# Loading q and k nine rows of a head at a time, and putting the rows back in order after the transposes

## The chip, the cores and the metric

The kernel runs on one core of one Trainium2 chip. The metric is the device time of one execution in microseconds (us). Executions agree within about 1%, so differences of a few us are judged on several runs taken in alternation with the kernel before. "Span" is the time from the first to the last instruction in the profiled execution; it is about 2 us shorter than the device time.

In what follows PE is the matrix engine, DVE the vector engine, ACT the scalar engine, POOL the GpSimd engine and SP the sync engine. DMA engines move data between the chip's main memory (HBM) and SBUF, the memory that the compute engines work from; PSUM is where PE leaves its results. A piece is a contiguous run of bytes that a load leaves in SBUF, and a packet is one entry of the trace's record of what the DMA engines moved; here each piece of q and k is one packet.

## The reference, cut to what matters

```python
# q, k, v: [8 batches, 8 heads, 576 rows, 64] float32;  w_phi: [64, 128]
proj = x @ w_phi                                   # for q and for k
proj = proj - max(abs(proj), axis=-1)
phi  = concatenate([exp(proj), exp(-proj)])        # 256 features
kv, z = sum_s phi_k * v,  sum_s phi_k
attn  = (phi_q @ kv) / (phi_q @ z + 1e-6)          # x: [8, 576, 512]
X = rfft(x, axis=1)[:, :64]                        # 64 modes
Y = X * (w_r + 1j*w_i)                             # w_r, w_i: [64, 512, 512] float32, 134 MB together
u = x + irfft(Y);  out = u + relu(u @ w_ch)
```

## The kernel before

One core does everything. 16 units (4 groups of two heads x 4 pairs of batches) go through the attention; a software pipeline overlaps three units. The spectral weights arrive in 64 groups, each of two 512 KB loads (bf16 after the cast in the load), in eight buffers plus five borrowed places, and are used ("mixed") between the pieces of the attention from the fifth unit on. POOL issues every load that casts float32 to bf16: k, q and the weights, in program order.

```python
def load(t, src, g, bp, eng):            # k, q by POOL; v by SP
    for i in range(2):                   # batch of the pair
        hs = src[2 * bp + i, 2 * g:2 * g + 2]
        eng.dma_start(                   # rows 4p..4p+3 on partition p
            t[:, 8 * i:8 * i + 8, :].rearrange("p (h c) d -> p h (c d)", h=2),
            hs[:, 0:512, :].rearrange("h (p c) d -> p h (c d)", c=4))
        eng.dma_start(                   # the other 64 rows
            t[64 * i:64 * i + 64, 16:18, :],
            hs[:, 512:576, :].rearrange("h p d -> p h d"))
# [cut] turn(): nine 128x128 transposes on PE, two ACT copies out of PSUM
# [cut] the attention of a unit; then, behind the attention and interleaved with it:
def wload(g, mg):
    wt = home(g, mg)
    for i, w in ((0, moe_w_r), (1, moe_w_i)):
        pool.dma_start(wt[:, i], w[mg*MG:(mg+1)*MG, g*128:(g+1)*128, :].rearrange("m p e -> p m e"))
    return wt
# [cut] the output stage: for each pair of batches nine chunks of 128 rows, and
            if n in (3, 7):
                nc.sync.dma_start(       # 1 MB, 128 partitions
                    out[2 * bp + n // 4, 0:512, :].rearrange("(p c) e -> p c e", c=4),
                    of[n // 4])
```

A q or k load thus leaves 512 B per piece in SBUF (four rows of 64 bf16) and the remainder loads 128 B.

## Time and profile before

| what | before |
|---|---|
| device time, median of the first 3 runs | 490.25 us |
| span | 488.5 us |
| load stage (start to the first matmul of the output stage) | 447.5 us |
| output stage (from there to the end) | 41.0 us |
| waits of PE for k | 25.0 us |

The last row is from the view of waits (engine, its output tile and line, what it waited for, us in total, times, longest; `one` is a tile in PSUM, L38 the line of a helper that issues every operation):

```profile
PE one L38 <- DMA kb<-in_k_dram: 25.0, 9, 8.7
```

The page of the kernel before gives the engines' busy tenths in 40 slices of 12.2 us, the data moved in each slice, the packets by queue (q0 is POOL's, q1 is SP's), and the chain of work that ended last:

```profile
PE   2772787778887887787696629676667767656994
...
DVE  5776569779767877868859544752222112100874
...
DMA  9999999999999999999999999999999999992576
GB/s 170 193 216 216 203 214 206 200 203 155 218 218 213 143 205 213 183 204 207 210 190 176 218 165 205 206 207 206 207 206 214 213 213 217 213 214 45 226 296 252
DMA packets 112341, 98.63 MB, mean 202 GB/s; under 512 B 17968, under 2 KB 110768, under 8 KB 111280
...
q0 software_dynamic: 94736, 77.09, 100.5%
q1 hardware_dynamic: 17568, 21.04, 14.5%
...
DMA 40%; DVE 23%; PE 22%; ACT 5%; issue 4%; POOL 3%; another core or an unknown queue 0%; DVEq 0%; SPq 0%; ACTq 0%; POOLq 0%
```

The DMA row is full through slice 36 (about 440 us); the rows of PE and DVE, the busiest compute engines, are not. The chain agrees: 40% of the span is DMA. So the load stage is a transfer stage. The GB/s row counts bytes written (bf16), and about 210 is what the loads reach at most of the time. The row has dips below it (155, 143, 183, 176, 165), which the prediction reads as holes in which the DMA engines ran short of work. The DMA digits can't show them, since packets overlap, but the packet records do: the packets that started in the microsecond from 164 us took 0.28 us of 16 engines' time, where the stretch with weights alone (330 to 350 us) has 1.24.

The transfers by tile in the same kernel (issuing queue, number of loads, KB each, median us from issue to landing):

```profile
out_dram<-of SPq DMA_DIRECT2D x8, 1024.0 KB, 3.9
kb<-in_k_dram POOLq DMA_DIRECT2D x32, 128.0 KB, 12.0
qb<-in_q_dram POOLq DMA_DIRECT2D x32, 128.0 KB, 7.9
...
kb<-in_k_dram POOLq DMA_DIRECT2D x32, 16.0 KB, 11.6
```

Each unit takes four loads for k and four for q. From the view of the tile that collects the output sums, the first and last start of its matmuls (us) show where the output stage begins:

```profile
L596 PE MATMUL pt<-xs,ident_b x36: 376/379/631, 447.5 to 480.8; 128*128 128x512 bf16 x36
```

The packet count of q0 agrees exactly with arithmetic: 64 weight groups, the channel weights, k and q make 90,624 data packets, and 257 loads by POOL add one 4-byte completion packet on each of 16 engines (257 x 16 = 4,112): 94,736 together.

### The profile page before, as it was taken

Reading aid. Unit: us, or ns where it says so; the run is one execution under the profiler, and the core shown is the slowest. Engines: PE = TensorE matmul, PEld = TensorE weight load, DVE = VectorE, ACT = ScalarE, POOL = GpSimd, SP = SyncE. Lnnn points to the kernel's source line nnn. Section 1 sums busy time; section 2 is a strip of 40 time slices with the busy share of each in tenths; the row PEclk is TensorE's granted clock in tenths of the full one; section 3 lists DMA queues with packets and bytes.
Section 4 is the critical chain, followed back from the end, with each engine's and each line's share of the span. In section 5 each row is a group of like instructions: output and inputs, shape, how many; then the busy total and the mean of one; then the engine's idle time right before and its main releaser. Section 6 shows DMA issues by size and latency. Waiting matters only on the chain.

```text
span 488.5 us, 8037 instructions
## 1 busy us (share of the span) xinstructions
PE 347.6 (71%) x3104; PEld 212.3 (43%) x3133; DVE 284.4 (58%) x492; ACT 256.8 (53%) x435; POOL 181.7 (37%) x267
## 2 busy tenths in 40 slices
PE   2772787778887887787696629676667767656994
PEld 1451655555565555554464416442333333322441
DVE  5776569779767877868859544752222112100874
ACT  3770866866966875765575717421213323210763
POOL 8754344647442642644255244232332323100000
PEclk9996958888977986978788957778999999975998
DMA  9999999999999999999999999999999999992576
GB/s 170 193 216 216 203 214 206 200 203 155 218 218 213 143 205 213 183 204 207 210 190 176 218 165 205 206 207 206 207 206 214 213 213 217 213 214 45 226 296 252
DMA packets 112341, 98.63 MB, mean 202 GB/s; under 512 B 17968, under 2 KB 110768, under 8 KB 111280
## 3 DMA queue, kind: packets, MB, share of 16 engines
q0 software_dynamic: 94736, 77.09, 100.5%
q1 hardware_dynamic: 17568, 21.04, 14.5%
q8 instruction: 24, 0.39, 0.3%
q14 instruction: 13, 0.11, 0.1%
HBM read 163.64 MB, written 9.44 MB: 354 GB/s over the span
## 4 chain that ended last, share of the span: by engine, by line
DMA 40%; DVE 23%; PE 22%; ACT 5%; issue 4%; POOL 3%; another core or an unknown queue 0%; DVEq 0%; SPq 0%; ACTq 0%; POOLq 0%
DMA wt<-in_moe_w_i_dram 28%; PE one L38 12%; DMA wt<-in_moe_w_r_dram 9%; DVE va L38 6%; DVE mq L38 4%; PE pt L596 4%; DVE nd L38 4%; DVE mk L38 4%; DMA kb<-in_k_dram 3%; DVE xs L38 3%; PE two L38 3%; POOL wt L38 3%; PE pt L598 3%; ACT AB L38 2%; DVE rd L38 1%
## 5 line engine op out<-in xcount | busy, mean ns | idle before, releaser
L38 ACT ACTIVATE AB<-two 128x1024 bf16<-128x1024 f32 x64 | 62.1, 1022 | 50.7 <-DVE mk L38 50.3
L38 ACT ACTIVATE AQ<-two 128x1024 bf16<-128x1024 f32 x64 | 62.5, 1038 | 18.0 <-PE two L38 12.3
L38 POOL DMA_DIRECT2D wt<-in_moe_w_r_dram x59 | 44.7, 758 | 66.8 <-DMA wt<-in_moe_w_r_dram 29.1
L38 POOL DMA_DIRECT2D qb<-in_q_dram x64 | 42.2, 666 | 73.4 <-DMA wt<-in_moe_w_i_dram 31.1
L38 POOL DMA_DIRECT2D wt<-in_moe_w_i_dram x59 | 44.5, 754 | 53.9 <-DMA wt<-in_moe_w_i_dram 48.8
L38 PE MATMUL one<-va,AB 128*128 128x65 bf16 x512 | 45.8, 223 | 17.5 <-DVE va L38 17.3
L465 ACT CAST xw<-one 128x512 bf16<-128x512 f32 x36 | 21.1, 586 | 67.4 <-PE one L463 51.2
L38 POOL DMA_DIRECT2D kb<-in_k_dram x64 | 42.3, 672 | 38.3 <-DMA wt<-in_moe_w_i_dram 17.9
L460 DVE COPY xT<-one 128x512 bf16<-128x512 bf16 x36 | 15.3, 425 | 61.8 <-PE one L458 61.1
L463 PE MATMUL one<-wchb,xT 128*128 128x512 bf16 x135 | 38.2, 397 | 14.5 <-DVE xT L460 14.0
L38 DVE TENSOR_REDUCE mk<-two 128x8 f32<-128x1024 f32 x32 | 39.0, 1219 | 5.8 <-PE two L38 5.8
L38 DVE TENSOR_TENSOR va<-vn,ee 128x1152 bf16<-128x1152 f32 x32 | 42.0, 1355 | 0.0
L38 PEld LDWEIGHTS <-AB 128*128 128x128 bf16 x512 | 29.1, 112 | 27.3 <-DVE va L38 11.9
L38 DVE TENSOR_REDUCE mq<-two 128x8 f32<-128x1024 f32 x32 | 37.7, 1217 | 1.4 <-PE two L38 1.4
L38 PE MATMUL one<-kvz,AQ 128*128 128x65 bf16 x512 | 29.6, 205 | 6.9 <-ACT kvz L38 2.7
L38 PE MATMUL one<-ident_b,kb 128*128 128x128 bf16 x144 | 14.4, 244 | 25.3 <-DMA kb<-in_k_dram 24.4
L38 PEld LDWEIGHTS <-AQ 128*128 128x128 bf16 x512 | 25.7, 105 | 15.1 <-issue 12.1
L38 PE MATMUL one<-CF,xs 128*128 128x256 bf16 x160 | 30.9, 364 | 1.7 <-DVE xs L38 1.7
L38 PE MATMUL one<-wt,XT_70 128*32 128x512 bf16 x256 | 22.5, 427 | 13.0 <-DMA wt<-in_moe_w_i_dram 8.9
L38 DVE TENSOR_TENSOR nd<-one,nd 128x390 f32<-128x390 f32 x48 | 27.1, 565 | 5.4 <-PE one L38 0.5
L609 DVE TENSOR_TENSOR of<-pt,rl 128x512 f32<-128x512 f32 x32 | 21.8, 690 | 13.8 <-ACT rl L607 13.4
L38 PE MATMUL two<-w2blk,qT 128*128 128x256 bf16 x128 | 19.8, 289 | 13.0 <-ACT AB L38 10.6
(124 smaller groups left out, 638.0 us busy)
## 6 DMA issues: line engine op xcount, KB each, us to landing
wt<-in_moe_w_r_dram POOLq DMA_DIRECT2D x59, 512.0 KB, 15.6
wt<-in_moe_w_i_dram POOLq DMA_DIRECT2D x59, 512.0 KB, 17.8
vn<-in_v_dram SPq DMA_DIRECT2D x32, 256.0 KB, 7.3
out_dram<-of SPq DMA_DIRECT2D x8, 1024.0 KB, 3.9
kb<-in_k_dram POOLq DMA_DIRECT2D x32, 128.0 KB, 12.0
qb<-in_q_dram POOLq DMA_DIRECT2D x32, 128.0 KB, 7.9
vn<-in_v_dram SPq DMA_DIRECT2D x32, 32.0 KB, 7.5
yacc<-in_moe_w_r_dram POOLq DMA_DIRECT2D x2, 512.0 KB, 6.9
```

The source lines that it names most:

```text
L38: ins = f(*args, **kwargs)
L460: nc.vector.tensor_copy(xT, pt)
L463: nc.tensor.matmul(pf, lhsT=xT[:, g, :], rhs=wchb[:, g, :], start=(g == 0), stop=(g == 3))
L465: nc.scalar.copy(xw[:, bp, n, :], pf)
L596: nc.tensor.matmul(po, lhsT=ident_b, rhs=base, start=True, stop=False)
L598: nc.tensor.matmul(p, lhsT=CI[:, n % 4, :], rhs=src[:, 2 * bp + n // 4, :], start=False, stop=True)
L609: nc.vector.tensor_tensor(out=o, in0=ps[0], in1=rl, op=ALU.add)
```

## The change

The intent is fewer and longer packets. With nine rows of a head on a partition, 576 = 64 x 9 rows fit on 64 partitions, the two batches fill 128, and there is no remainder load: 1,152 B per piece and two loads instead of four for each of k and q. The price is that the transposes deliver rows in another order, so the ACT copies out of PSUM put them back into chunks of 128 rows, and v, the Fourier tables and the output take the new row order (row 9p + 4u + c on partition 64u + p), which splits v's loads and the output's stores into halves of 64 partitions.

The main parts of the edit:

```diff
         def load_v(self):
             self.vn = pin.tile([128, 18, D_], F32, name="vn")
-            load(self.vn, v, self.g, self.bp, sp)
+            for i in range(2):
+                vs = v[2 * self.bp + i, 2 * self.g:2 * self.g + 2].rearrange(
+                    "h (p r) d -> p h r d", r=9)
+                for u in range(2):
+                    sp.dma_start(
+                        self.vn[64 * u:64 * u + 64, 8 * i:8 * i + 8, :].rearrange(
+                            "p (h c) d -> p h (c d)", h=2),
+                        vs[:, :, 4 * u:4 * u + 4, :].rearrange("p h c d -> p h (c d)"))
+                sp.dma_start(self.vn[64 * i:64 * i + 64, 16:18, :], vs[:, :, 8, :])
+
+        def load_wide(self, src, name):
+
+            t = pin.tile([128, 2, 10, D_], BF16, name=name)
+            for h in range(2):
+                pool.dma_start(
+                    t[:, h, 0:9].rearrange("p r d -> p (r d)"),
+                    src[2 * self.bp:2 * self.bp + 2, 2 * self.g + h].rearrange(
+                        "b (p r) d -> b p (r d)", r=9))
+            return t
 
         def turn(self, src, name):
 
-            dst = pm.tile([128, 9, 128], BF16, name=name, tag="xT", bufs=3)
-            flat = src.rearrange("p n d -> p (n d)")
-            for lo, hi in ((0, 4), (4, 9)):
-                ptr = one([128, hi - lo, 128], BF16)
-                for j in range(lo, hi):
-                    pe.transpose(ptr[:, j - lo, :], flat[:, j * 128:(j + 1) * 128], ident_b)
-                act.copy(dst[:, lo:hi, :], ptr)
-            return dst
+            dst = pm.tile([128, 2, 2, 2, 2, 64], BF16, name=name, tag="xT", bufs=3)
+            rest = pm.tile([128, 2, 128], BF16, name=name + "r", tag="xTr", bufs=3)
+            flat = src.rearrange("p h r d -> p h (r d)")
+            for h in range(2):
+                ptr = one([128, 6, 128], BF16)
+                for j in range(4):
+                    pe.transpose(ptr[:, j, :], flat[:, h, j * 128:(j + 1) * 128], ident_b)
+                if h == 1:
+                    for hh in range(2):
+                        pe.transpose(ptr[0:64, 4 + hh, :], flat[:, hh, 512:576], ident_b)
+                act.copy(
+                    dst[:, h].rearrange("p m b u s -> p u (m b) s"),
+                    ptr[:, 0:4].rearrange("p (u m) (b s) -> p u (m b) s", u=2, b=2))
+                if h == 1:
+                    act.copy(rest[0:64], ptr[0:64, 4:6])
+            return dst, rest
```

In the attention code (cut): the projection of the remainder rows takes two matmuls of 64 input rows instead of one of 128 for `rows`, and one instead of two for `cols`; the sums over k accumulate in another order. The output:

```diff
             if n in (3, 7):
-                nc.sync.dma_start(
-                    out[2 * bp + n // 4, 0:512, :].rearrange("(p c) e -> p c e", c=4),
-                    of[n // 4])
+                rows = out[2 * bp + n // 4].rearrange("(p r) e -> p r e", r=9)
+                for u in range(2):
+                    nc.sync.dma_start(
+                        rows[:, 4 * u:4 * u + 4, :], of[n // 4][64 * u:64 * u + 64])
         for i in range(2):
-            nc.sync.dma_start(out[2 * bp + i, 512:576, :], ofr[64 * i:64 * i + 64, :])
+            rows = out[2 * bp + i].rearrange("(p r) e -> p r e", r=9)
+            nc.sync.dma_start(rows[:, 8, :], ofr[64 * i:64 * i + 64, :])
```

More of the change, by code (lines that the diff above doesn't have):

```diff
@@ L88 @@
     pm = pm_cm.__enter__()
-    def load(t, src, g, bp, eng):
-        for i in range(2):
-            hs = src[2 * bp + i, 2 * g:2 * g + 2]
-            eng.dma_start(
-                t[:, 8 * i:8 * i + 8, :].rearrange("p (h c) d -> p h (c d)", h=2),
-                hs[:, 0:512, :].rearrange("h (p c) d -> p h (c d)", c=4),
-            )
-            eng.dma_start(
-                t[64 * i:64 * i + 64, 16:18, :],
-                hs[:, 512:576, :].rearrange("h p d -> p h d"),
-            )
     class Unit:
@@ L108, in load_k @@
         def load_k(self):
-            self.kb = pin.tile([128, 18, D_], BF16, name="kb")
-            load(self.kb, k, self.g, self.bp, pool)
+            self.kb = self.load_wide(k, "kb")
         def load_q(self):
-            self.qb = pin.tile([128, 18, D_], BF16, name="qb")
-            load(self.qb, q, self.g, self.bp, pool)
+            self.qb = self.load_wide(q, "qb")
         def load_v(self):
             self.vn = pin.tile([128, 18, D_], F32, name="vn")
-            load(self.vn, v, self.g, self.bp, sp)
@@ L142, in rows @@
                 ps = two([128, 8, 128])
-                for j in range(4):
-                    if by_head:
-                        o = ps[:, 2 * j:2 * j + 2, :]
-                    else:
-                        h, cc = j // 2, j % 2
-                        o = ps.rearrange("p (c h) f -> p c h f", h=2)[:, 2 * cc:2 * cc + 2, h, :]
-                    pe.matmul(o, lhsT=tT[:, 4 * i + j, :],
-                              rhs=w2blk.rearrange("p (c f) -> p c f", c=2),
-                              start=True, stop=True)
+                o = ps.rearrange("p (h m e) f -> p h m e f" if by_head
+                                 else "p (m e h) f -> p h m e f", h=2, m=2)
+                for h in range(2):
+                    for m_ in range(2):
+                        pe.matmul(
+                            o[:, h, m_],
+                            lhsT=tT[0][:, h, m_, i].rearrange("p u s -> p (u s)"),
+                            rhs=w2blk.rearrange("p (e f) -> p e f", e=2),
+                            start=True, stop=True)
             else:
                 ps = one([128, 2, 128])
-                pe.matmul(ps.rearrange("p h f -> p (h f)"), lhsT=tT[:, 8, :], rhs=w2blk,
-                          start=True, stop=True)
+                for h in range(2):
+                    pe.matmul(ps[:, h, :], lhsT=tT[1][0:64, h, :], rhs=w2blk[0:64, 0:128],
+                              start=True, stop=True)
             n = slice(8 * i, 8 * i + 8) if i < 2 else slice(16, 18)
@@ L193, in kv @@
             pk = one([128, 4, 65])
-            for h in range(2):
-                for ab in range(2):
-                    o = pk[:, 2 * h + ab, :]
-                    for c in range(4):
-                        pe.matmul(
-                            o, lhsT=self.AB[i][:, ab, 4 * h + c, :],
-                            rhs=self.va[:, ab, 8 * i + 4 * h + c, :],
-                            start=(c == 0), stop=False,
-                        )
-                    r = slice(64 * i, 64 * i + 64)
+            hab = [(h, ab) for h in range(2) for ab in range(2)]
+            for h, ab in hab:
+                for c in range(4):
                     pe.matmul(
-                        o, lhsT=self.AB[2][r, ab, h, :], rhs=self.va[r, ab, 16 + h, :],
-                        start=False, stop=True,
-                    )
+                        pk[:, 2 * h + ab, :], lhsT=self.AB[i][:, ab, 4 * h + c, :],
+                        rhs=self.va[:, ab, 8 * i + 4 * h + c, :],
+                        start=(h == ab == c == 0), stop=False,
+                    )
+            r = slice(64 * i, 64 * i + 64)
+            for h, ab in hab:
+                pe.matmul(
+                    pk[:, 2 * h + ab, :], lhsT=self.AB[2][r, ab, h, :],
+                    rhs=self.va[r, ab, 16 + h, :], start=False, stop=(h == ab == 1),
+                )
             act.copy(self.kvz[:, i], pk)
@@ L219, in cols_q @@
             if i < 2:
-                ps = two([128, 2, 4, 128])
-                for c2 in range(2):
+                ps = two([128, 2, 2, 2, 128])
+                for e in range(2):
                     pe.matmul(
-                        ps[:, c2].rearrange("p n s -> p (n s)"),
-                        lhsT=w2blk[:, c2 * 128:(c2 + 1) * 128],
-                        rhs=self.qT[:, 4 * i:4 * i + 4, :].rearrange("p n s -> p (n s)"),
+                        ps[:, e], lhsT=w2blk[:, e * 128:(e + 1) * 128],
+                        rhs=self.qT[0][:, :, :, i].rearrange("p h m u s -> p h m (u s)"),
                         start=True, stop=True,
@@ L229, in cols_q @@
                 ps = one([128, 2, 128])
-                for h in range(2):
-                    pe.matmul(ps[:, h, :], lhsT=w2blk[:, h * 128:(h + 1) * 128],
-                              rhs=self.qT[:, 8, :], start=True, stop=True)
+                pe.matmul(ps, lhsT=w2blk[0:64, 0:128], rhs=self.qT[1][0:64],
+                          start=True, stop=True)
             self.pa = ps
@@ L238, in exp_q @@
             if i < 2:
-                t = pm.tile([128, 2, 2, 4, 128], BF16, name="AQ")
+                t = pm.tile([128, 2, 2, 2, 2, 128], BF16, name="AQ")
             else:
@@ L256, in num @@
                             pn[ab][:, n - n0, :],
-                            lhsT=self.AQ[i][:, ab, c % 2, 2 * h + c // 2, :],
+                            lhsT=self.AQ[i][:, ab, c % 2, h, c // 2, :],
                             rhs=self.kvz[:, i, 2 * h + ab, :], start=True, stop=True,
@@ L305 @@
     si = const.tile([128, 5], I32, name="si")
-    pool.iota(si[:, 0:4], [[1, 4]], base=0, channel_multiplier=4)
-    pool.iota(si[0:64, 4:5], [[1, 1]], base=512, channel_multiplier=1)
-    pool.iota(si[64:128, 4:5], [[1, 1]], base=512, channel_multiplier=1)
+    for u in range(2):
+        pool.iota(si[64 * u:64 * u + 64, 0:4], [[1, 4]], base=4 * u, channel_multiplier=9)
+        pool.iota(si[64 * u:64 * u + 64, 4:5], [[1, 1]], base=8, channel_multiplier=9)
     mi = const.tile([128, 64], I32, name="mi")
@@ L610 @@
             if n in (3, 7):
-                nc.sync.dma_start(
-                    out[2 * bp + n // 4, 0:512, :].rearrange("(p c) e -> p c e", c=4),
-                    of[n // 4])
+                rows = out[2 * bp + n // 4].rearrange("(p r) e -> p r e", r=9)
+                for u in range(2):
+                    nc.sync.dma_start(
+                        rows[:, 4 * u:4 * u + 4, :], of[n // 4][64 * u:64 * u + 64])
         for i in range(2):
-            nc.sync.dma_start(out[2 * bp + i, 512:576, :], ofr[64 * i:64 * i + 64, :])
+            rows = out[2 * bp + i].rearrange("(p r) e -> p r e", r=9)
+            nc.sync.dma_start(rows[:, 8, :], ofr[64 * i:64 * i + 64, :])
     pb_cm.__exit__(None, None, None)
```

## The prediction

> **What bounds the kernel now.** The transfers. On the page all slices up to about 440 us show the DMA engines at nine tenths or more while no compute engine stays there. The chain of waits gives DMA 40% of the span, nearly all of it from 217 us to 442 us and nearly all weights (wt). Before that the chain runs through DVE, PE and ACT at about 17.5 us a unit; after 447 us some 41 us of output remain, which the change hardly touches. The waits view shows POOL waiting 160 us in all for earlier weight loads to land before it may issue the next load, so DMA work saved is mostly time saved.
>
> **Packet costs.** The trace's packet records: a 1 KB weight packet takes 98 ns, a 512 B k/q packet 60, a 128 B one 32. Packets overlap: in the weights-only stage 4,014 packets start per 20 us on 16 engines, so one costs an engine about 80 ns. Scaling, my estimates are 48 ns for 512 B and 26 ns for 128 B.
>
> **Removed.** q and k are now 16,384 + 8,192 packets (50 + 13 us of all 16 engines). After: 8,192 packets of 1,152 B, estimated at 87 ns, 44.5 us. With 64 fewer completions that is about 19 us less DMA work. POOL issues 64 loads instead of 128 (670 ns each).
>
> **How much is on the path.** Until the first mix (108 us) compute sets the pace: the 13 weight groups loaded ahead just finish there, so the saving for units 0 to 6 is lost. Nine units remain, 1.2 us each: 11 us. Second, the DMA has short holes in the attention stage (around 112-116, 165-170, 247, 264 and 292 us, some 9 us together), where POOL's limited number of loads in flight consists of small q and k pieces. Half as many pieces should fill most holes. Third, the waits of PE for kb (16 us from 240 to 290 us) shrink with it.
>
> **Added.** Per turn one more ACT copy (existing ones 604-766 ns, so about 0.25 us net), one more transpose, per unit one more rows matmul for each of q and k; about 0.3 us per unit, partly hidden. v and the output are halved into 64 partitions: same packets, more issues (SP has time); a slight slowdown of v is possible.
>
> **A doubt.** The new loads have the batch (2) as outermost source dimension. The Trainium skill, "DMA: Bandwidth & Descriptors", section "Why a DMA increments its semaphore by 16 and not by 1", says the engine count divides the outermost dimension of both sides; then each q/k load runs on 2 of 16 engines (64 x 87 ns = 5.6 us) and 8 loads cover all. Nothing in the trace before shows this. Total work is unchanged, but engines go out of step by up to 5.6 us and first units start 1 to 2 us later. I count 3 us for it.
>
> **Sum.** 11 + 6 saved, less 3 for uneven engines, less 3 for added compute and v: about 11 us, so 479 us (range 467 to 490). Faster by over 2% 0.56, within 2% 0.39, slower 0.05.
>
> **Right if:** q0 packets fall from 94,736 to about 77,300; the last weight lands near 430 us instead of 442; the span of the output stage stays at 41 us; POOL's DMA busy time halves for qb and kb; PE's waits for kb shrink.
>
> **Wrong if:** rows of 1,152 B cost far more than 87 ns or are split; two-engine loads delay weights and kb, with PE waiting for kb longer than before; 64-partition v loads slow down; or units grow by more than 0.5 us, so that compute, not DMA, sets the pace and the saving turns into idle DMA.

## The result, and the profile after

The changed kernel takes 510.88 us (median of 4 runs, 507.64 to 512.73) against 490.7 us for the kernel before in the same comparison: ratio 1.0416, 95% interval 1.0346 to 1.0485, so 4% slower. A ratio is the mean time of one kernel's fast runs over that of the other's of the same rounds, so it is not quite the ratio of the medians. Executions over 1.5% slower than the fastest of the same kernel are left out of the means. The prediction (479, 467 to 490) missed.

The same lines of the page after:

```profile
PE   0674776786967497698558739766676767639990
...
DVE  4379488778777857967748656661221222103770
...
DMA  7999999999999999999999999999999999961997
GB/s 112 188 188 199 208 200 206 197 202 133 198 205 212 171 188 211 190 201 196 207 201 178 219 181 201 206 206 207 206 207 213 216 213 216 211 126 34 258 252 214
DMA packets 152918, 98.87 MB, mean 194 GB/s; under 512 B 66736, under 2 KB 151344, under 8 KB 151856
...
q0 software_dynamic: 134672, 77.31, 99.5%
q1 hardware_dynamic: 18208, 21.05, 16.2%
...
DMA 70%; PE 14%; DVE 5%; issue 3%; ACT 3%; POOL 2%; DVEq 0%; POOLq 0%; ACTq 0%
```

Two things stand out. The DMA row is still full and the chain is now 70% DMA. And q0 does not have the predicted 77,300 packets but 134,672, more than before, although the bytes are the same: "under 512 B" went from 17,968 to 66,736.

```profile
vn<-in_v_dram SPq DMA_DIRECT2D x64, 128.0 KB, 7.6
out_dram<-of SPq DMA_DIRECT2D x16, 512.0 KB, 5.8
kb<-in_k_dram POOLq DMA_DIRECT2D x32, 144.0 KB, 15.7
qb<-in_q_dram POOLq DMA_DIRECT2D x32, 144.0 KB, 14.2
```

```profile
L606 PE MATMUL pt<-xs,ident_b x36: 376/379/631, 460.0 to 493.9; 128*128 128x512 bf16 x36
```

The output stage starts at 460.0 us, 12.5 us later than before, and lasts 508.6 - 460.0 = 48.6 us, 7.6 us longer. So there are two losses, in two stages. (The half-size stores take 5.8 us to land, where the whole ones took 3.9.)

What the extra packets are, the trace's packet records say: 60,432 packets of POOL's queue are 4 B long. 129 of POOL's loads (the weights) account for 16 each, 2,064 together. The rest, 58,368, is 64 x 912, so every q or k load has 912 of them. And 912 = 14 x 64 + 16. A load of 128 pieces carried by two engines gives each 64 pieces; the count fits if each of the other 14 engines gets 64 four-byte packets in their place, and all 16 one completion packet. (By the same arithmetic a load carried by four engines would have 12 x 32 + 16 = 400.) The records do not name the engine, so the two engines are inferred from the count. The Trainium skill, "DMA: Bandwidth & Descriptors", section "Why a DMA increments its semaphore by 16 and not by 1", states the rule that gives two: the engine count must divide the slowest dimension of both sides, and the source here has the batch, 2, outermost. The page does not mention the four-byte packets.

### The profile page after: what moved, and what is told of

Read it like the earlier page. It is cut to its first block, busy times and chain, and to the rows that moved or that the text cites. A ratio compares the mean times of both kernels' runs of the same rounds, so it can differ in the third digit from the quotient of the medians.

```text
span 508.6 us, 8127 instructions
## 1 busy us (share of the span) xinstructions
PE 345.0 (68%) x3168; PEld 203.7 (40%) x3181; DVE 286.0 (56%) x492; ACT 260.6 (51%) x467; POOL 149.6 (29%) x204
## 3 DMA queue, kind: packets, MB, share of 16 engines
q0 software_dynamic: 134672, 77.31, 99.5%
## 4 chain that ended last, share of the span: by engine, by line
DMA 70%; PE 14%; DVE 5%; issue 3%; ACT 3%; POOL 2%; DVEq 0%; POOLq 0%; ACTq 0%
DMA wt<-in_moe_w_r_dram 22%; DMA wt<-in_moe_w_i_dram 22%; DMA kb<-in_k_dram 12%; DMA qb<-in_q_dram 7%; PE one L38 5%; DMA xs<-in_moe_w_r_dram 4%; PE pt L606 4%; DMA yacc<-in_moe_w_r_dram 3%; PE pt L608 3%; ACT AB L38 1%; DVE va L38 1%; DVE nd L38 1%; PE two L38 1%; POOL kb L38 1%; DVE mk L38 1%
## 5 line engine op out<-in xcount | busy, mean ns | idle before, releaser
L38 PE MATMUL one<-ident_b,kb 128*128 128x128 bf16 (+1 forms) x160 | 19.8, 275 | 48.3 <-DMA kb<-in_k_dram 48.0
L38 ACT COPY kT<-one 128x512 bf16<-128x512 bf16 x32 | 18.4, 597 | 43.7 <-PE one L38 42.9
L38 PE MATMUL one<-va,AB 128*128 128x65 bf16 x512 | 30.9, 226 | 13.5 <-DVE va L38 13.5
L38 POOL DMA_DIRECT2D qb<-in_q_dram x32 | 25.4, 797 | 46.9 <-DMA wt<-in_moe_w_i_dram 14.6
L38 POOL DMA_DIRECT2D kb<-in_k_dram x32 | 26.2, 821 | 37.1 <-PE one L38 14.0
L38 PEld LDWEIGHTS <-AB 128*128 128x128 bf16 x512 | 27.0, 120 | 18.6 <-issue 12.2
L38 PEld LDWEIGHTS <-kb 128*128 128x128 bf16 (+1 forms) x160 | 12.4, 121 | 54.9 <-DMA kb<-in_k_dram 50.9
L38 PEld LDWEIGHTS <-AQ 128*128 128x128 bf16 x512 | 23.8, 104 | 22.0 <-issue 19.5
```

The lines of the kernel that those rows point to most:

```text
L38: ins = f(*args, **kwargs)
```

## The experiments

Each kernel was timed in three rounds in alternation with the kernel before. "Load stage" and "output stage" are as defined above, from the profiled execution. The third column sums the duration of all packets that started before the last weight packet ended, divided by 16 engines; packets on one engine overlap, so it exceeds the elapsed time, and only its changes matter. It is my sum over the trace's packet records. The stage figures are each from one execution: between kernels whose loads are the same (before, e3, e4 and e5; or e1, e6 and e7) the load stage scatters by up to 2 us.

| kernel | load stage, us | packet time, us | of it 4 B packets of POOL | output stage, us | median, us | ratio to before |
|---|---|---|---|---|---|---|
| before | 447.5 | 538.3 | 4.7 | 41.0 | 490 | 1 |
| after | 460.0 | 555.1 | 40.2 | 48.6 | 510.88 | 1.0416 |
| e1_by_batch | 432.4 | 511.7 | 3.7 | 47.1 | 480.99 | 0.9814 |
| e2_before_batch_outer | 466.2 | 570.5 | 36.7 | 41.8 | 507.61 | 1.0355 |
| e3_before_out_halves | 446.9 | 538.7 | 4.7 | 48.6 | 496.56 | 1.0131 |
| e4_before_out_rows | 445.6 | | | 40.8 | 489.54 | 1.0000 |
| e5_before_out_evenodd | 446.2 | | | 42.5 | 491.82 | 1.0029 |
| e6_by_batch_two_queues | 431.3 | | | 44.8 | 478.11 | 0.9764 |
| e7_interleaved | 432.1 | 511.7 | 3.7 | 42.8 | 476.92 | 0.9730 |
| e8_after_out_whole | 461.8 | 553.7 | 38.9 | 43.2 | 506.82 | 1.0340 |
| e9_q_by_head | 448.5 | 539.0 | 20.7 | 49.0 | 498.47 | 1.0178 |
| e10_k_by_head | 449.2 | 538.0 | 20.9 | 49.0 | 500.23 | 1.0191 |

### e1_by_batch: the change with 64 as the outermost source dimension

```diff
-            for h in range(2):
-                pool.dma_start(
-                    t[:, h, 0:9].rearrange("p r d -> p (r d)"),
-                    src[2 * self.bp:2 * self.bp + 2, 2 * self.g + h].rearrange(
-                        "b (p r) d -> b p (r d)", r=9))
+            for b in range(2):
+                pool.dma_start(
+                    t[64 * b:64 * b + 64, :, 0:9].rearrange("p h r d -> p h (r d)"),
+                    src[2 * self.bp + b, 2 * self.g:2 * self.g + 2].rearrange(
+                        "h (p r) d -> p h (r d)", r=9))
```

> The changed kernel, but each q/k load takes one batch and both heads (64 partitions, outermost source dimension 64) instead of one head and both batches (outermost source dimension 2). Same number of loads, same 8,192 packets of 1,152 B. Theory A (batch-outermost loads run on two engines and make the other 14 carry 64 four-byte packets each): the four-byte packets of q0 fall from 60,432 to about 3,100, the load stage ends about 20 us earlier, time about 488 us, with the output stage still at 48 us. Rival B (rows of 1,152 B, 64-partition tiles or the added copies and matmuls are what costs): 505 us or more.

Measured: 480.99 us, ratio 0.9814 (0.9773 to 0.9854), faster by just under 2% and correct; that is 7 us below the expected 488, and the gain in the load stage was 27.6 us, not about 20. The same bytes land in the same places in the same number of pieces and loads; only which pieces share a load differs. From the page of this kernel and its views of transfers and of the output tile:

```profile
DMA  8999999999999999999999999999999999952997
GB/s 152 216 217 214 211 212 212 219 210 155 217 214 211 218 219 206 219 219 208 218 219 209 217 206 207 205 207 207 207 214 212 213 213 213 213 98 55 270 265 211
...
q0 software_dynamic: 77328, 77.08, 96.6%
```

```profile
out_dram<-of SPq DMA_DIRECT2D x16, 512.0 KB, 5.8
kb<-in_k_dram POOLq DMA_DIRECT2D x32, 144.0 KB, 14.6
```

```profile
L606 PE MATMUL pt<-xs,ident_b x36: 376/379/631, 432.4 to 465.7; 128*128 128x512 bf16 x36
```

q0 has 77,328 packets, the predicted "about 77,300" and exactly what the arithmetic gives (90,624 - 24,576 + 8,192 data packets and 193 x 16 completions). The load stage ends 27.6 us before that of the changed kernel and 15.1 us before that of the kernel before. The dips in the GB/s row between slices 11 and 24 are gone (in e6 and e7 too, while e3, e4 and e5 keep them), which was the second gain of the prediction. One dip is left (155, in the tenth slice): the stretch where the weight groups loaded ahead are done and the first mix, at 109.5 us, has not yet freed a buffer. There the saving of the first units turns into idle DMA, as predicted. The output stage is still 47.1 us, so it is a separate matter. Rival B falls: the longer pieces, 64-partition tiles, added copies and added matmuls all are in this kernel, and its load stage is the better one.

### e2_before_batch_outer: the outermost dimension alone, in the kernel before

Shortened:

```diff
+        # q and k only; v keeps its two loads
+            for h in range(2):
+                eng.dma_start(
+                    t[:, 16 + h, :],
+                    src[2 * bp:2 * bp + 2, 2 * g + h, 512:576, :])
```

The two remainder loads of 16 KB took one batch and both heads; here they take one head and both batches.

> The kernel before, but the two small remainder loads of q and k take one head and both batches (batch outermost) instead of one batch and both heads. Same number of loads and data packets. Theory A: 58,000 more four-byte packets, some 25 us more DMA work, time about 510 us, although no other part of the change is there. Rival B: 490 us, as before.

Measured: 507.61 us, ratio 1.0355 (1.0297 to 1.0414), 2.4 us under the expected 510. POOL's queue has 152,080 packets, 57,344 more than before (64 loads x 896):

```profile
q0 software_dynamic: 152080, 77.32, 103.2%
```

```profile
L603 PE MATMUL pt<-xs,ident_b x36: 376/379/631, 466.2 to 500.4; 128*128 128x512 bf16 x36
```

Nothing else of the change is present. These loads carry 16 KB where those of the change carry 144, and they still cost 18.7 us of load stage and 32.0 us of packet time in four-byte packets (36.7 - 4.7; the change: 36.5 over e1_by_batch). So the four-byte packets go with the number of pieces (128 a load) and the outermost dimension, not with the bytes.

### e9_q_by_head and e10_k_by_head: late k, or busy DMA engines?

A rival was still open. The changed kernel's PE waits much longer for k. The view of waits of the changed kernel, then of e1_by_batch:

```profile
PE one L38 <- DMA kb<-in_k_dram: 48.0, 12, 12.8
```

```profile
PE one L38 <- DMA kb<-in_k_dram: 12.1, 2, 7.8
```

One could say that a two-engine load of k is simply late, and that this is the loss. Then q, which PE hardly waits for, should be harmless. The edit, shortened:

```diff
+            if name == "qb":        # e9; "kb" in e10
                 # as in the change: one head, both batches
+            else:
+                # as in e1_by_batch
```

> The changed kernel with k loaded by batch (outermost source dimension 64) and only q still with the batch outermost. Theory A (the four-byte packets cost time on all DMA engines): half of them, about 31,800, so about half of the loss comes back: first output matmul at about 446 us, time 494 to 497 us, although PE's wait for kb shrinks to about that of e1_by_batch (12 us). Rival F (the loss is that kb lands late and PE waits for it, 48 us in the changed kernel against 12 us in e1_by_batch; q is hardly ever waited for): about 481 us.

> The mirror of e9: q loaded by batch, only k still with the batch outermost. Theory A: about the same as e9, 494 to 497 us. Rival F (late kb is the loss): about 510 us, as the changed kernel.

Measured: 498.47 us (ratio 1.0178, 1.0117 to 1.0239) and 500.23 us (1.0191, 1.0113 to 1.0269): the same within the noise, both somewhat past the middle between e1_by_batch and the changed kernel. Rival F needed 481 and 510. Part of the expectation missed. The two are 1.5 and 3.2 us above the range given, and in e9 PE's wait for kb was 27.7 us, not 12, although k is loaded there as in e1_by_batch. So k was late in e9 too, and e9 alone would not clear it. What does is that the length of this wait does not set the load stage. In e4 (below), whose loads are those of the kernel before, it was 9.4 us instead of 25.0, and the load stage is 445.6 us against 447.5:

```profile
PE one L38 <- DMA kb<-in_k_dram: 9.4, 3, 7.1
```

Nor is it the time that POOL needs to issue these loads. POOL was busy for 149.6 us in the changed kernel and for 135.7 in e1_by_batch, but for 181.7 in the kernel before, whose load stage is shorter than the changed kernel's; and in the changed kernel it waited more for transfers to land (203.9 us in all, against 162.5 in e1_by_batch).

What is left is occupation of the DMA engines, and the packet records show it. I counted from start and duration how many packets were in flight. Between 15 and 300 us of the changed kernel it was 19.9 on average, as many as in its stretch with weights alone (330 to 350 us, 19.9), so the engines were no less busy; but only 17.8 of them were data (over 4 B), against 19.1 of 19.4 in e1_by_batch. And the loss builds up only while q and k are loaded: against e1_by_batch, the 500th 1 KB packet of POOL's queue ended 5 us later, the 20,000th 17 us, the 40,000th (at 316.0 us) 27.5 us, and the 66,000th still 27.7 us.

### e3, e4, e5: what lengthens the output stage

Three edits of the kernel before, shortened, each turning one 1 MB store into two of 512 KB. In the expectations, C is the theory that a store from 64 partitions is slower, C1 that it matters which 64, and C2 that any 64 are slow:

```diff
-                nc.sync.dma_start(rows, of[n // 4])                     # 128 partitions
+    # e3    rows[64*u:64*u+64]    <- of[n // 4][64*u:64*u+64]           # lower, upper 64 partitions
+    # e4    rows[:, 2*u:2*u+2, :] <- of[n // 4][:, 2*u:2*u+2, :]        # 128 partitions, two rows each
+    # e5    even partitions, then odd partitions                        # 64 partitions
```

> The kernel before, each 1 MB output store split into two stores of 64 partitions. Theory C (a store that reads 64 partitions runs slower): output stage 41 us becomes about 48 us, time about 497 us, 8 KB packets take 450 ns or more instead of 321. Rival D (the row pitch of 18 KB in HBM is what slows the stores of the changed kernel): 490 us, packets 321 ns.

> The kernel before, each 1 MB output store split into two stores of 128 partitions and two rows (4 KB pieces). Theory C: about 490 to 492 us, output stage 41 to 43 us. Rival E (twice the number of stores is what costs): about 497 us, as the split by partitions.

> The kernel before, each 1 MB output store split into two stores of 64 partitions again, but the even and the odd partitions instead of the lower and the upper 64. Theory C1 [...]: about 490 us, output stage 41 to 43 us, 8 KB packets near 321 ns. Rival C2 (64 partitions in a store are slow in themselves[...]): 497 us, as the split into lower and upper halves.

Measured: e3 496.56 us (ratio 1.0131, 1.0077 to 1.0186), e4 489.54 (1.0000, 0.9932 to 1.0068), e5 491.82 (1.0029, 0.9975 to 1.0084). In the view of transfers the stores of e3 and of e5, equal in number, size and number of partitions, differ by how long they take to land:

```profile
out_dram<-of SPq DMA_DIRECT2D x16, 512.0 KB, 5.9
```

```profile
out_dram<-of SPq DMA_DIRECT2D x16, 512.0 KB, 3.5
```

The 8 KB packets took 477 ns on average in e3, 321 in e5 and 321 in the kernel before (487 in the changed kernel). So it is not the number of stores (e4 has as many), not 64 partitions as such (e5), and not the row pitch of 18 KB in the output (e3 has none of it; e5 writes at a pitch of 16 KB and is not slow): it is which 64. A little may be left for the number 64: e5's stores landed in 3.5 us, e4's, of the same size from 128 partitions, in 2.6, and the output stage of e5 is 42.5 us against 40.8. The Trainium skill, "SBUF — State Buffer", section "Door 1: The DMA port swizzle (why `[64,N]` ≈ `[32,N]`)", says that partitions 0 to 63 reach only 8 of 16 ports; by the port formula given there the even partitions reach all of them. These runs agree with it: 5.9 against 3.5 us. That the ports are the reason is the page's account; the runs show only that the choice of partitions decides.

### e6_by_batch_two_queues: both halves at once

```diff
-                    nc.sync.dma_start(
+                    (nc.sync, nc.scalar)[u].dma_start(
                         rows[:, 4 * u:4 * u + 4, :], of[n // 4][64 * u:64 * u + 64])
```

> e1_by_batch with the upper-half stores of the output issued by ACT, so that lower and upper half can be in flight together. Theory C1: most of the 6 us of the output stage come back, time about 476 us, although the stores are the same. Rival: the stores keep their pace (or ACT's issues delay the relu), 481 us or more.

Measured: 478.11 us, ratio 0.9764 (0.9715 to 0.9813); output stage 44.8 us instead of 47.1. About 40% of the 6 us comes back, less than expected. The 8 KB packets still take 443 ns on average (median 334), which would fit halves that overlap only part of the time; no run shows that.

### e7_interleaved: rows interleaved over the partitions

Shortened:

```diff
-            dst = pm.tile([128, 2, 2, 2, 2, 64], BF16, ...)      # ... b u s: column 64u + s
+            dst = pm.tile([128, 2, 2, 2, 64, 2], BF16, ...)      # ... b s u: column 2s + u
-                for u in range(2):                               # output, v alike
-                    nc.sync.dma_start(rows[:, 4*u:4*u+4, :], of[n // 4][64*u:64*u+64])
+                nc.sync.dma_start(                               # 128 partitions in one store
+                    rows[:, 0:8, :].rearrange("p (u c) e -> p u (c e)", u=2),
+                    of[n // 4].rearrange("p c e -> p (c e)"))
```

Row 9p + 4u + c goes to partition 2p + u. The outermost dimension is 64 on one side and 128 on the other, and all 128 partitions are in one transfer. The frequency tables are built for this order by a few small DVE instructions.

> e1_by_batch with the two halves of rows interleaved over the partitions (row 9p+4u+c on partition 2p+u instead of 64u+p), so that v and the output move 128 partitions in one transfer. Candidate that should beat both kernels. Theory C1: output stage 41 us, load stage as in e1_by_batch (432 us): about 474 us, if the ACT copies with a step of two elements stay near 600 ns. If these copies get slow (over 1 us), the attention stage grows and the gain is lost: 480 us or more.

Measured: 476.92 us (476.64 to 477.15), correct, ratio 0.9730 (0.9692 to 0.9768): it beats both kernels, though it is 3 us above the expected 474. The output stage is 42.8 us, not 41, and the load stage 432.1. The ACT copies with a step of two elements got slower, 744 and 833 ns instead of 600 and 674 in e1_by_batch, without an effect on the load stage. v is loaded in halves in e1_by_batch and whole here, and the load stages agree within 0.3 us (1 KB packets of SP's queue 59 ns in both), so the halves of v cost nothing that these runs show.

### e8_after_out_whole: the two losses add up

```diff
-                for u in range(2):
-                    nc.sync.dma_start(rows[:, 4*u:4*u+4, :], of[n // 4][64*u:64*u+64])
+                nc.sync.dma_start(
+                    out[2 * bp + n // 4, 0:512, :].rearrange("(p c) e -> p c e", c=4), of[n // 4])
```

Its output is wrong, which doesn't matter for the time.

> The changed kernel with the output stores of before (128 partitions, wrong row order, so a wrong result on purpose); all else, the two-engine loads too, as in the change. Theory: the output stage falls from 48.6 us to 41 to 42 us and nothing else moves: about 504 us. Rival (output and loads are not additive, or the row pitch in HBM matters): another number; 510 us if the stores cost nothing.

Measured: 506.82 us, ratio 1.0340 (1.0299 to 1.0382). The output stage falls to 43.2 us (5.4 of the 7.6 us), the load stage stays at 461.8 with all its four-byte packets. The time is nearly 3 us above the expectation; 1.8 of it lie in a load stage that I took to be unchanged.

## Why the prediction was wrong

- **The bound was right.** The load stage is a transfer stage before and after, and its length grows with the packet time in the kernels of the table, though not in proportion and with a scatter of a few us: 511.7, 538.3, 555.1 and 570.5 us of packet time go with 432.4, 447.5, 460.0 and 466.2 us.
- **The savings were about right.** With the engine count put right (e1_by_batch), the load stage is 15.1 us shorter; the prediction had 11 us for packets plus 6 for holes. The 1,152 B pieces took 107 ns (median) where the 1 KB ones take 98, so the estimate of 87 ns of an engine holds up, and the holes after the first mix vanished. How the 15.1 us split between the two was not measured.
- **The step that failed: "Total work is unchanged, but engines go out of step ... I count 3 us for it."** The prediction saw that the loads may run on two engines, and costed only the unevenness. The two-engine form is not free of work for the others: 912 four-byte packets a load, 40.2 us of packet time against 3.7, which is 36.5 of the 43.4 us by which the changed kernel's packet time exceeds that of e1_by_batch. The term put at 3 us measured 27.6 us (load stage of the changed kernel less that of e1_by_batch), some 5 us of it before the first unit is under way. The same order of dimensions alone, in the 16 KB loads of the kernel before, cost 18.7 us (e2). The expected 77,300 packets of q0, written as a check, failed at once (134,672) and pointed to the cause. The prediction had "two-engine loads delay weights and kb" among its ways to be wrong, but gave "slower" only 0.05.
- **A second step failed: "the span of the output stage stays at 41 us."** It grew to 48.6, because each store reads the lower or the upper 64 partitions. "v and the output are halved into 64 partitions: same packets" was true and not enough: the same packets took 487 ns instead of 321. For v, the same worry turned out to be nothing.
- **Added compute was probably over-counted.** ACT's busy time rose from 256.8 us to 259.7 in e1_by_batch and 260.6 in the changed kernel, 3 to 4 us in all rather than 8 (0.25 us for each of 32 turns). What that cost in time was not measured; in e7 ACT was busy for 265.8 us and the load stage was no longer than in e1_by_batch.
- **The waits of PE for kb grew** from 25.0 to 48.0 us instead of shrinking; in e1_by_batch they were 12.1, which is the direction of the prediction but within the scatter: with the loads of the kernel before they were 25.0, 21.7 (e3), 19.3 (e5) and 9.4 (e4). The longest in the changed kernel, 12.8 us, is the first: the first unit starts 7 us later than before (the first wait was 5.8 us there), not the 1 to 2 us of the prediction.

Sum in stages: 490.7 before, -15.1 for the pieces, +27.6 for the batch outermost, +7.6 for the output (6.1 of it already in e1_by_batch), which is 510.8; measured 510.88. This is no independent check: the terms are differences of the same profiled spans, so they add up by construction to the difference of two executions, and only the agreement with the medians, to a tenth, is left, which is luck.

What stays open: half of the batch-outermost loads (e9, e10) cost 16.1 and 16.8 us of load stage, more than half of 27.6. The four-byte packets explain 17.0 of the 27.3 us of additional packet time in e9; the rest is that weight, v and q/k packets take slightly longer. In e2, whose loads on two engines are small, that rest is missing: 32.0 of its 32.2 us of additional packet time are four-byte packets. Engines that stood idle because others lagged, which is what the prediction's "out of step" would mean, the packet counts do not show: in the changed kernel fewer than 16 packets were in flight for under 1% of the time from 15 to 300 us. But the records do not name the engines, and no kernel here has loads on two engines without the four-byte packets, so the two were not separated by a run.

## What to carry to other kernels

Before fusing two loads into one, read the access pattern of the source from its outermost dimension: a 2 there made a load of 128 pieces cost time of DMA engines that, by the packet count, carry none of it, and regrouping the same pieces so that 64 came first turned a loss of 4% into a gain of just under 2%. Where a layout splits a tile over partitions, try interleaving the parts (2p + u) instead of stacking them (64u + p), so that one transfer still covers all 128 partitions; here that took 4.3 us off the output stage (e7 against e1_by_batch). And count packets after a change of layout: a number that does not match the arithmetic (here 912 per load) led to the cause before any timing did.

## What the Trainium skill lacked or had wrong

- "DMA: Bandwidth & Descriptors", section "Why a DMA increments its semaphore by 16 and not by 1": its rule for the engine count fits these runs, and "all 16 engines post the +1" does too (16 completions a load), but it does not say that a load issued by POOL on two engines also sends four-byte packets: 912 four-byte packets per load of 128 pieces instead of 16 (9 ns each, median; 60,432 in all in the queue).
- The same page, section "Rules for kernel authors", row "Use all 16 engines", speaks of confining that one DMA; it gives no cost for the other traffic. Here 64 such loads of 128 pieces cost 18.7 us of load stage when they carried 16 KB (e2) and 27.6 us when they carried 144 KB.
- "SBUF — State Buffer", section "Door 1: The DMA port swizzle (why `[64,N]` ≈ `[32,N]`)": right for stores (8 KB packets 477 ns from stacked halves, 321 ns from even and odd partitions). It does not say when the limit is not felt: v's float32 loads into 64 partitions, mixed with the weights, showed no loss (59 ns per 1 KB packet halved and whole).
- The same page, section "Can I just issue two DMAs to hit both halves?", says that only one transfer spanning all 128 partitions reaches all ports. The packets of a store from the 64 even or odd partitions took no longer than those of one from 128 (8 KB packets 321 ns in both, e5), though the store of 512 KB landed in 3.5 us where one from 128 partitions took 2.6 (e4). Lower and upper halves issued from two queues recovered about 40% of the loss (e6).
